# Attention prologue of a two-layer-type kernel: loads of x first on one queue, LayerNorm ahead of the head moves, mask rows filled by token halves, four PSUM banks in one ring

## The chip, the cores and the metric

The kernel runs on one NeuronCore of a Trainium2 chip. A core has engines that run their own instruction streams: TensorE (PE, matmuls and transposes), VectorE (DVE), ScalarE (ACT), GpSimd (POOL) and SyncE (SP, which here only issues DMAs). They meet through semaphores. PE reads SBUF and writes PSUM, which has eight banks of 2 KB per partition. DMAs are issued from the queues of SP, ACT and POOL and share 16 DMA engines. The metric is device time in microseconds (us), median of several runs.

## The reference, cut to what matters

x has 2048 tokens of 576 features. Four layers, A, B, A, B, each added to x. A is attention over a sliding dilated window: 32 heads of 18 features, each token sees the tokens 0, 2, 4, ... 14 behind it. B is a gated MLP that mixes tokens with a 2048 x 2048 matrix; the change does not touch it.

```python
def _A_ref(x, wqkv, wo):
    ...
    W, dil = (8, 2)
    qkv = (lambda x, *d: x.transpose(*d))((x @ wqkv).reshape(B, S, 3, H, Dh), 2, 0, 3, 1, 4)
    q, k, v = (qkv[0], qkv[1], qkv[2])
    ...
    idx = pos[:, None] - off[None, :]
    mask = idx >= 0
    ...
    logits = jnp.einsum('bhsd,bhswd->bhsw', q, kg) * scale
    logits = jnp.where(mask[None, None, :, :], logits, -1000000000.0)
    attn = _softmax(logits, axis=-1)
    o = jnp.einsum('bhsw,bhswd->bhsd', attn, vg)
    return (lambda x, *d: x.transpose(*d))(o, 0, 2, 1, 3).reshape(B, S, D) @ wo
...
x = x + _A_ref(_layernorm(x, axis=-1), A_wqkv, A_wo)
x = x + _B_ref(_layernorm(x, axis=-1), B_w_in, B_w_sp, B_b_sp, B_w_out)
```

(and the last two lines a second time). Inputs and output are bf16.

## The kernel before

Layers are numbered 0 to 3; 0 and 2 are A, 1 and 3 are B. An A layer is written out by hand: inside `manual_schedule` (L336) each engine runs its instructions in the order in which the program makes them. Tokens come in 16 tiles of 128. The normalised x is kept transposed in `xnT` (features on partitions, 16 padding columns in front).

**Stages of an A layer.**
- LayerNorm. In layer 0, `x_load` brings x in as bf16, four tiles at most in a load (tiles 8 to 11 into memory of `oT`, under the name `spare`, the last four into the buffer of the first four). `LNX_stats` takes two bn_stats and one aggregate per tile on VectorE, adds eps, and lets GpSimd raise it to the power -0.5 (L505). `LNX_apply` writes (x - mean) * rstd on VectorE into one of four buffers `ln_xn` (L513). Tiles 0 to 3 are transposed on PE (L518) and copied by ScalarE, the rest by DMA transposes on SP (`ln_T`, L245). Before them, 40 matmuls of an identity by itself (`warm`, L493) run on PE. In layer 2, x was normalised at the end of layer 1.
- `VW(t, hh)` makes half of the values of one of 19 query tiles of 112 tokens: five matmuls of 288 columns, evacuated into `v_ext` (L361).
- `PG(d, qk, cc)`, a projection group, makes q (qk 0) or k (qk 1) of seven heads (four for d = 4) for 512 tokens `cc`: five matmuls of 512 columns into a PSUM bank `pp` (L383), evacuated by ScalarE or VectorE into a staging buffer `stg` (L353, L355). When the four parts of a `stg` (q and k, two cc) are there, one DMA per head moves its 18 rows to that head's place in `QK`: these are the head moves (L392, shown as L77). There are three staging buffers in layer 0, four in layer 2, used in turn; a group can be evacuated only when the moves out of its buffer have landed. The queues of the moves are taken in turn from `q2`, two thirds GpSimd and one third SP.
- The window is imposed by adding rows to q and k: each head has 32 partitions in `QK`, 18 of features and 14 of a pattern with a period of 256 tokens. `build_window_rows` makes a period, sends it through DRAM (`win_period`) into `win_pat`, and `fill_window_rows` copies it over all of `QK` on VectorE, two of eight head groups at a time; the head moves then write over 18 of each 32 rows, so they come after the fill.
- Attention runs in 38 steps `s`, two per query tile (half of the heads each): `L_mm(s)`, 16 logits matmuls into two double banks (`L_ps`, L407), `EXP(s)` on ScalarE (L416), `PV(s)`, 16 matmuls into a bank `O_ps` (L427), a reciprocal and a product on VectorE into `o_t`, and every second step a DMA transpose on SP into `oT` (L438). A table says what else is issued at which step: the remaining groups and values, `WO(i, hh)` (the output projection, bank `pw`, L453), the store of x, LayerNorm for layer B, and loads of B's weights. L_mm(s + 1) and EXP(s + 1) are issued before PV(s).

**PSUM.** Four banks are two double banks `H` (logits). Of the other four, two carry the tag `O` (O_ps) and two the tag `PT` (pp, pv, pw); users that don't mind take the two tags in turn (`PT_tile`, L194). A tile waits for whoever had its bank last.

**Order in layer 0's prologue.** x of tiles 0 to 7 on SP; the weights of v, then of q and k (`wqk`) on ACT's queue; window rows; identity; warm matmuls; LayerNorm of tiles 0 to 3, VW of three tiles, LayerNorm of 4 to 7, loads of x for 8 to 15, the whole fill, then ten pairs of groups (the first 1024 tokens), with LayerNorm of tiles 8 to 11 after the fourth pair and of 12 to 15 after the fifth. Then four more groups (tokens 1024 to 1535 of d = 0, 1, L588) and L_mm(0).

**Order in layer 2.** The ten pairs of groups, with the fill and `setup_bufs` (zeroing padding of `P_sb` and `o_t` on GpSimd, ones into `v_ext` on ScalarE) after the first; VW(0); four groups; L_mm(0).

Memory comes from stacks of pools: `main` first, then `sb`. The staging buffers are in `sb`. A tile that takes memory of an earlier one waits until that one has been read for the last time.

Of the kernel before, what the change touches and what calls it, by code (L numbers as in the profile page):

```python
# [18 lines left out]
P = 128  # L19
D = 576  # L20
H = 32
# [41 lines left out]
class K:  # L63
# [24 lines left out]
    def setup(self):  # L88
# [18 lines left out]
        self.pt_rr = 0  # L107
# [8 lines left out]
    def build_window_rows(self, c):  # L116
# [8 lines left out]
        self.pat = self.consts.tile([P, 2, 256], bf16, name="win_pat")  # L125
# [41 lines left out]
        self.dma(one[:].rearrange("a r (p f) -> p (a r) f", f=16), R[0:16].rearrange("p a r f -> p (a r) f"))  # L167

        def load(eng):
            for j in range(4):  # L170
                self.dma(self.pat[32 * j + DH:32 * j + 32, :, :], one[:].rearrange("a r x -> r a x"), eng=eng)
# [10 lines left out]
    def fill_window_rows(self, QK, g0, g1):  # L182
        nc, S, n = self.nc, self.cfg.S, g1 - g0
        for a in range(2):
            nc.vector.tensor_copy(out=QK[:, a, g0:g1, 0:S].rearrange("p g (k x) -> p g k x", x=256),
                                  in_=self.pat[:, a, None, None, :].to_broadcast([P, n, S // 256, 256]))
            nc.vector.tensor_copy(out=QK[:, a, g0:g1, S:S + PADL],
                                  in_=self.pat[:, a, None, 0:PADL].to_broadcast([P, n, PADL]))
        nc.vector.tensor_copy(out=QK[:, 1, g0:g1, 0:PADL], in_=self.patpad[:, None, :].to_broadcast([P, n, PADL]))
# [4 lines left out]
    def PT_tile(self, shape, dt, name, any_bank=True):  # L194
        self.pt_rr += 1
        tag = "O" if any_bank and self.pt_rr % 2 else "PT"
        return self.ps.tile(shape, dt, name=name, tag=tag, bufs=2)

    def O_tile(self, shape, dt, name):
        return self.ps.tile(shape, dt, name=name, tag="O", bufs=2)  # L200
# [113 lines left out]
    def layer_A(self, li):  # L314
# [9 lines left out]
        qT, kT = QK[:, 0], QK[:, 1]  # L324
        v_ext = main.tile([P, NT, H, DH + 1], bf16, name="v_ext")
# [18 lines left out]
        def setup_bufs():  # L344
            for pb in P_bufs:
                nc.gpsimd.memset(pb[:, :, :, QT:P], 0.0)
            for ob_ in o_bufs:
                nc.gpsimd.memset(ob_[:, D:640], 0.0)
            nc.scalar.copy(out=v_ext[:, :, :, DH:DH + 1], in_=self.ones[:, None, None, :].to_broadcast([P, NT, H, 1]))
# [7 lines left out]
        def VW(t, hh, dve):  # L357
            nk = tdim(t)[0]
            pv = self.PT_tile([P, 512], f32, "pv", any_bank=False)
# [6 lines left out]
        NSTG = 3 if li == 0 else 4  # L366
        CBW = 1024
        dma_rr = [0]

        def PG(d, qk, cc, dve, queues=(nc.sync, nc.gpsimd)):  # L370
# [4 lines left out]
            if key not in stg_tiles:  # L375
                stg_tiles[key] = sb.tile([P, 2, CBW], bf16, name="stg", tag="stg", bufs=NSTG)
                stg_left[key] = 2 * (CBW // 512)
            stg = stg_tiles[key]
            pp = self.PT_tile([P, 512], f32, "pp", any_bank=False)
# [39 lines left out]
        def PV(s):  # L419
            t, hf = divmod(s, 2)  # L420
            nk, nq = tdim(t)
            O_ps = self.O_tile([P, 512], f32, "O_ps")
# [23 lines left out]
        def WO(i, hh):  # L446
# [4 lines left out]
            pw = self.PT_tile([P, 512], f32, "pw", any_bank=False)  # L451
# [20 lines left out]
        if li == 0:  # L472
# [12 lines left out]
            self.load_wqk(nc.scalar)  # L485
            x_load(x1[:, 0:4, :], 4, 4, nc.sync)
            self.zero_right()
            self.build_window_rows(sb)
            self.load_pat(nc.sync)
            self.make_ident()  # L490
            warm = self.PT_tile([P, 512], f32, "warm", any_bank=False)
            for _ in range(40):
                nc.tensor.matmul(warm[:, 0:P], lhsT=self.ident[:], rhs=self.ident[:], start=True, stop=True)  # L493
            setup_bufs()

            def LNX_stats(i0, n):
                mv = sb.tile([P, 4, 2], f32, name="lnx_mv", tag="lnx_mv", bufs=2)
                for k_ in range(n):
# [34 lines left out]
            for t in range(3):  # L533
                for hh in range(2):
                    VW(t, hh, False)
# [426 lines left out]
```

The softmax here doesn't subtract the row's maximum and nothing guards it: scores larger than these inputs give would overflow.

## Time and profile before

| | us |
|---|---|
| median of 7 runs | 1234.35 |
| lowest, highest | 1233.11, 1239.22 |
| profiled execution, its own time | 1234.35 |
| its span, first to last instruction | 1232.5 |
| PE busy in it | 1195.5 |
| mean granted PE clock | 0.993 |

Busy time by stretch of the span, from a view that cuts it into windows (0 to 160 is layer 0, 160 to 625 layer 1, 625 to 762 layer 2, the rest layer 3):

| stretch, us | length | PE busy | PE clock | DMA share |
|---|---|---|---|---|
| 0 to 47 | 47 | 36.00 | 0.96 | 0.66 |
| 47 to 60 | 13 | 8.77 | 0.87 | 0.50 |
| 60 to 125 | 65 | 57.49 | 0.97 | 0.88 |
| 125 to 165 | 40 | 39.53 | 1.00 | 0.80 |
| 165 to 640 | 475 | 472.81 | 1.00 | 0.25 |
| 640 to 665 | 25 | 21.93 | 0.87 | 0.29 |
| 665 to 705 | 40 | 37.14 | 1.00 | 0.90 |
| 705 to 762 | 57 | 54.70 | 1.00 | 1.02 |
| 762 to 805 | 43 | 43.00 | 1.00 | 1.06 |
| 805 to 1140 | 335 | 335.00 | 1.00 | 0.04 |
| 1140 to 1232.5 | 92.5 | 89.12 | 1.00 | 0.36 |

Times are us, and ns where a line says mean. PE stands for matmuls, PEld for the loading of weights, SPq for SP's queue. "L383" is the line of the kernel. "pp<-xnT,wqk_sb" reads: written tile, then what was read. A time in brackets with an arrow is the idle time of that engine before the instruction and what ended it; "issue" means that nothing in the profile shows what it waited for. The DMA share is the mean busy share of the 16 DMA engines.

### The profile page before, as it was taken

How to read it: one execution, taken by the hardware profiler on the slowest of the kernel's cores; microseconds unless marked ns; L12 is line 12 of the kernel's file. 1: busy time of each engine (PE TensorE's matmuls, PEld its weight loads, DVE VectorE, ACT ScalarE, POOL GpSimd, SP SyncE). 2: the span in 40 equal slices, each digit the busy share in tenths (PEclk: the TensorE clock that was granted, in tenths of full speed). 3: DMA queues.
4: the chain of work that ended last, by engine and by line, in shares of the span. 5: the costliest groups of instructions: out<-in, count | busy, mean ns of one | idle time of the engine just before them, and what ended most of it. 6: DMA issues, size and time to landing. Idle time of an engine off the chain costs nothing. (4 is left out here: it accounts for less than half of the span.)

```text
span 1232.5 us, 20796 instructions
## 1 busy us (share of the span) xinstructions
PE 1195.5 (97%) x8568; PEld 623.8 (51%) x8568; DVE 545.4 (44%) x1206; ACT 385.4 (31%) x605; POOL 275.8 (22%) x380
## 2 busy tenths in 40 slices
PE   7789999999999999999999999999999999999998
PEld 4346744444444444447754576444444444444577
DVE  8347867533332322334453577674332232332321
ACT  5457867501011011101146586772001101111000
POOL 3447676300000000001152577751000000000000
PEclk9899999999999999999998999999999999999999
DMA  6688987000000000046644898920000000000432
GB/s 181 110 158 189 198 188 166 22 1 11 11 11 12 1 11 11 1 154 191 173 102 96 179 229 178 243 60 22 1 11 11 11 11 11 12 1 2 135 109 73
DMA packets 176149, 101.58 MB, mean 82 GB/s; under 512 B 134954, under 2 KB 156506, under 8 KB 176054
## 3 DMA queue, kind: packets, MB, share of 16 engines
q1 hardware_dynamic: 163814, 76.04, 28.0%
q0 software_dynamic: 6896, 18.39, 5.9%
q10 hardware_dynamic: 5344, 5.83, 1.5%
q8 instruction: 67, 1.10, 0.4%
q14 instruction: 28, 0.23, 0.1%
HBM read 42.39 MB, written 16.53 MB: 48 GB/s over the span
## 5 line engine op out<-in xcount | busy, mean ns | idle before, releaser
L795 PE MATMUL pg<-Wq,Z 128*128 128x512 bf16 x2304 | 502.8, 379 | 0.0
L795 PEld LDWEIGHTS <-Z 128*128 128x128 bf16 x2304 | 225.7, 98 | 271.6
L799 DVE TENSOR_TENSOR g_tmp<-pg,ln_xn 128x512 f32<-128x512 f32 x144 | 99.6, 692 | 429.1 <-PE pg L795 429.1
L789 ACT ACTIVATE z1T<-pz 128x1024 bf16<-128x1024 f32 x72 | 73.7, 1024 | 513.8 <-PE pz L777 513.6
L849 PE MATMUL po<-wout,Z 128*128 128x288 bf16 x1152 | 141.4, 286 | 0.0
L77 POOL DMA_DIRECT2D wout<-in_B_w_out_dram x4 | 4.3, 1064 | 604.6 <-PE pg L795 604.6
L416 ACT ACTIVATE P_sb<-L_ps 128x896 bf16<-128x896 f32 (+1 forms) x152 | 126.4, 887 | 41.3 <-PE L_ps L407 40.7
L777 PE MATMUL pz<-xnT,w 128*128 128x512 bf16 (+1 forms) x640 | 136.0, 380 | 0.0
L849 PEld LDWEIGHTS <-Z 128*128 128x128 bf16 x1152 | 112.7, 98 | 28.8
L700 PEld LDWEIGHTS <-xnT 128*128 128x128 bf16 (+1 forms) x800 | 66.3, 97 | 81.9 <-issue 24.5
L383 PE MATMUL pp<-xnT,wqk_sb 128*128 128x512 bf16 x400 | 98.5, 397 | 6.7 <-ACT stg L355 4.0
L700 PE MATMUL pz<-win2a,xnT 128*128 128x512 bf16 x384 | 104.4, 380 | 0.0
L800 DVE TENSOR_TENSOR Z<-g_tmp,z1T 128x512 bf16<-128x512 f32 x144 | 99.7, 692 | 9.7
L777 PEld LDWEIGHTS <-w 128*128 128x128 bf16 (+1 forms) x640 | 51.1, 97 | 80.0 <-issue 27.1
L714 ACT ACTIVATE zp<-pz 128x1024 bf16<-128x1024 f32 x64 | 65.5, 1024 | 44.9 <-PE pz L700 32.4
L238 POOL TENSOR_SCALAR ln_xn<-x_new,ln_mv,ln_rstd 128x576 bf16<-128x576 f32 x32 | 73.3, 2290 | 3.4
L859 DVE TENSOR_TENSOR x_new<-po,xo 128x288 f32<-128x288 f32 (+1 forms) x64 | 28.8, 456 | 87.8 <-PE po L849 87.8
L700 PE MATMUL pz<-win2b,xnT 128*128 128x512 bf16 (+1 forms) x256 | 65.7, 380 | 0.0
L383 PEld LDWEIGHTS <-wqk_sb 128*128 128x128 bf16 x400 | 38.3, 101 | 52.3 <-issue 16.4
L77 POOL DMA_DIRECT2D QK<-stg x74 | 48.4, 657 | 64.3 <-issue 26.1
L716 DVE CUSTOM_DVE_ANT_0 Z<-zp 128x1536 bf16<-128x1536 bf16 x32 | 56.9, 1779 | 11.2 <-ACT zp L714 11.2
L453 PE MATMUL pw<-wo_sb,oT 128*128 128x288 bf16 x320 | 49.1, 286 | 11.7 <-issue 4.8
(103 smaller groups left out, 903.2 us busy)
## 6 DMA issues: line engine op xcount, KB each, us to landing
xres<-x_new SPq DMA_DIRECT2D x48, 288.0 KB
xo<-xres SPq DMA_DIRECT2D x48, 288.0 KB
QK<-stg POOLq DMA_DIRECT2D x74, 72.0 KB, 3.9
wout<-in_B_w_out_dram POOLq DMA_DIRECT2D x4, 1296.0 KB, 9.4
w<-in_B_w_in_dram SPq DMA_DIRECT2D x16, 256.0 KB
QK<-stg SPq DMA_DIRECT2D x54, 72.0 KB
win2a<-in_B_w_in_dram POOLq DMA_DIRECT2D x12, 288.0 KB, 5.4
wqk_sb<-in_A_wqkv_dram ACTq DMA_DIRECT2D x2, 1152.0 KB
```

The lines of the kernel that those rows point to most:

```text
L238: e.tensor_scalar(out=xn[:nrows, 0:D], in0=x_t[:nrows, :], scalar1=mv[:nrows, 0:1], scalar2=rstd[:nrows, 0:1], op0=ALU.subtract, op1=ALU.mult)
L383: nc.tensor.matmul(pp[:, :], lhsT=w, rhs=self.xnT[:, c, PADL + cc * 512:PADL + (cc + 1) * 512], start=(c == 0), stop=(c == 4))
L416: nc.scalar.activation(out=P_bufs[(2 * s + jp) % 4][:nk, :, :, 0:nq], in_=Lv[:nk, :, :, 0:nq], func=ACT.Exp, scale=scale)
L700: nc.tensor.matmul(pzvs[ci][:, sub * 512:sub * 512 + w], lhsT=self.xnT[r0:r1, c, PADL + i * P:PADL + (i + 1) * P], rhs=win2(c)[r0:r1, c0 + ...
L714: nc.scalar.activation(out=zp[:, c0:c0 + cn], in_=pzvs[ci][:, 0:cn], func=ACT.Gelu_apprx_tanh, accum_out=sums[:, ci:ci + 1])
L716: nc.vector.tensor_tensor_reduce(out=spare[:, 0:SQ_D], in0=zp[:, 0:SQ_D], in1=zp[:, 0:SQ_D], scale=1.0, scalar=0.0, op0=ALU.mult, op1=ALU. ...
L777: nc.tensor.matmul(pz1s[q // 2][:, q % 2, :], lhsT=w1[r0:r1, c, sub * P:(sub + 1) * P], rhs=self.xnT[r0:r1, c, PADL + q * 512:PADL + (q + ...
L789: nc.scalar.activation(out=z1T[:, q2 * 512:(q2 + 2) * 512], in_=pz1s[q2 // 2][:, :, :].rearrange("p a b -> p (a b)"), func=ACT.Gelu_apprx_ ...
L795: nc.tensor.matmul(pg[:, :], lhsT=Z[:, jj, i, sub * P:(sub + 1) * P], rhs=Wq[q][:, i, :], start=(i == 0), stop=(i == NS - 1))
L799: nc.vector.tensor_tensor(out=tmp[:], in0=pg[:, :], in1=bsp[:, qs], op=ALU.add)
L800: nc.vector.tensor_tensor(out=uT(jj)[:, sub, qs], in0=tmp[:], in1=z1Ts[jj, sub][:, qs], op=ALU.mult)
L849: nc.tensor.matmul(acc[hh], lhsT=uT(j // 2)[:, j % 2, i * P:(i + 1) * P], rhs=wouts[j // NJH][:, j % NJH, hh * 288:(hh + 1) * 288], start= ...
```

## The change

- Loads: `wqk` moves from ACT's queue to SP, behind the x of tiles 0 to 7; x of tiles 8 to 11 comes next, ahead of the window pattern; x of 12 to 15 after the apply of tiles 4, 5. `win_period` is sent from ACT's queue. `load_wo` moves from step 1 to the prologue.
- LayerNorm of layer 0 is cut into statistics (S_), eps (E_), power on GpSimd (R_), apply (A_), transpose (T_pe, T_) and issued by hand, tile by tile. Statistics of all 16 tiles, and all but the power, apply and transpose of the last four, stand ahead of the groups; the power of tiles 12 to 15 comes after d = 1's head moves. `warm` has 26 matmuls.
- The fill is cut into two halves of 1024 tokens: the second is issued after the fifth pair of groups (layer 0) or the seventh (layer 2). A copy covers four head groups; the pattern gets a tail of 16 columns.
- Head moves of the first half in layer 0: d = 0, 1, 4 on GpSimd alone; d = 2, 3 on GpSimd and SP in turn.
- pp, pv, pw, O_ps and all other single-bank users share one ring of four banks.
- Staging buffers lie in `main`, behind `QK`.
- Groups of the second half: two, not four, come early, after EXP(0) and evacuated by VectorE; the other 18 are spread over 14 steps. VW of tiles up to 6 (layer 0) or 3 (layer 2) stand ahead of L_mm(0). WO of tiles 0 to 2 in layer 0 comes two steps later. B's first weights are loaded from step 4, not 2.
- An Exp of one column (`exp_table`) early in each A layer loads ScalarE's table; layer 2's `setup_bufs` and the ones of `v_ext` run on VectorE.

```diff
-        self.dma(one[:].rearrange("a r (p f) -> p (a r) f", f=16), R[0:16].rearrange("p a r f -> p (a r) f"))
+        self.dma(one[:].rearrange("a r (p f) -> p (a r) f", f=16), R[0:16].rearrange("p a r f -> p (a r) f"), eng=eng)
...
-    def fill_window_rows(self, QK, g0, g1):
...
+    def fill_window_rows(self, QK, half):
+        nc, n = self.nc, self.cfg.S // 2
+        if half == 0:
+            nc.vector.tensor_copy(out=self.pat[:, :, 256:272], in_=self.pat[:, :, 0:16])
+            nc.vector.tensor_copy(out=QK[:, 0, :, 0:PADL], in_=self.pat[:, 0, None, 0:PADL].to_broadcast([P, 8, PADL]))
+            nc.vector.tensor_copy(out=QK[:, 1, :, 0:PADL], in_=self.patpad[:, None, :].to_broadcast([P, 8, PADL]))
+        c0 = PADL + half * n
+        for g0 in (0, 4):
+            for a in range(2):
+                nc.vector.tensor_copy(out=QK[:, a, g0:g0 + 4, c0:c0 + n].rearrange("p g (k x) -> p g k x", x=256),
+                                      in_=self.pat[:, a, None, None, PADL:PADL + 256].to_broadcast([P, 4, n // 256, 256]))
...
+    def PT_tile(self, shape, dt, name):
+        return self.ps.tile(shape, dt, name=name, tag="PT", bufs=4)
...
+        stgs = [main.tile([P, 2, CBW], bf16, name=f"stg{k_}") for k_ in range(NSTG)]
...
+        def exp_table():
+            nc.scalar.activation(out=P_bufs[0][:, 0, 0, 0:1], in_=self.ones[:, 0:1], func=ACT.Exp)
...
             self.load_wv(nc.scalar)
-            self.load_wqk(nc.scalar)
             x_load(x1[:, 0:4, :], 4, 4, nc.sync)
+            self.load_wqk(nc.sync)
             self.zero_right()
+            exp_table()
...
+            x_load(spare, 8, 4, nc.sync)
             self.load_pat(nc.sync)
...
+            S_(0, 1)
+            E_(0, 2)
+            R_(0, 2)
+            S_(2)
+            A_(0, 1)
+            T_pe(0)
+            T_pe(1)
+            VW(0, 0, False)
+            VW(0, 1, False)
+            S_(3)
+            E_(2, 2)
+            R_(2, 2)
+            VW(1, 0, False)
+            VW(1, 1, False)
+            S_(4)
+            A_(2, 3)
+            T_pe(2)
+            T_pe(3)
+            S_(5)
+            E_(4, 2)
+            R_(4, 2)
+            VW(2, 0, False)
+            VW(2, 1, False)
+            S_(6)
+            A_(4, 5)
+            x_load(sb.tile([P, 4, D], bf16, name="x_in3", tag="x_in", bufs=2)[:], 12, 4, nc.sync)
+            T_(4, 5)
+            S_(7)
+            E_(6, 2)
+            R_(6, 2)
+            A_(6, 7)
+            T_(6, 7)
+            self.load_wo(nc.gpsimd)
+            self.fill_window_rows(QK, 0)
+            S_(8, 9, 10, 11)
+            E_(8, 4)
+            R_(8, 4)
+            A_(8, 9, 10, 11)
+            T_(8, 9, 10, 11)
+            S_(12, 13, 14, 15)
+            E_(12, 4)
             order = [(d, cc) for cc in (0, 1) for d in (0, 1, 2)] + [(d, cc) for d in (3, 4) for cc in (0, 1)]
             for k_, (d, cc) in enumerate(order):
                 for qk in (1, 0):
-                    PG(d, qk, cc, False, q2)
+                    PG(d, qk, cc, False, (nc.gpsimd, nc.sync) if 2 <= d <= 3 else (nc.gpsimd,))
                 if k_ == 4:
+                    R_(12, 4)
+                    A_(12, 13, 14, 15)
+                    self.fill_window_rows(QK, 1)
                 if k_ == 7:
+                    T_(12, 13, 14, 15)
+            nvw0, nvw = 3, 7
         else:
...
                 if k_ == 0:
+                    setup_bufs(nc.vector)
+                    nc.vector.memset(v_ext[:, :, :, DH:DH + 1], 1.0)
+                    self.fill_window_rows(QK, 0)
+                    exp_table()
                 if k_ == 1:
                     self.run_deferred()
+                if k_ == 6:
+                    self.fill_window_rows(QK, 1)
+            nvw0, nvw = 0, 4
...
+        for t in range(nvw0, nvw):
             for hh in range(2):
+                VW(t, hh, False)
...
-        for d, qk, cc in pgs[:4]:
-            PG(d, qk, cc, False, q2)
-        pgs = pgs[4:]
+        pre, pgs = pgs[:2], pgs[2:]
...
-            s = 2 * t + (4 if t < NT - 3 else 3)
+            s = 2 * t + (6 if li == 0 and i < 3 else 4 if t < NT - 3 else 3)
...
-            at(2 + 2 * k_, f)
+            at(4 + 2 * k_, f)
...
         L_mm(0)
         EXP(0)
+        for d, qk, cc in pre:
+            PG(d, qk, cc, True, q2)
```

## The prediction, made before the changed kernel had run

> **What bounds the kernel now.** I read the busy shares first, then the chain of waits, then what TensorE waits for, then TensorE, ScalarE and GpSimd in order of time around the two attention layers.
>
> ```profile
> PE 1195.5 (97%) x8568; PEld 623.8 (51%) x8568; DVE 545.4 (44%) x1206; ACT 385.4 (31%) x605; POOL 275.8 (22%) x380
> PE 42%; DMA 1%; DVE 0%; issue 0%; ACT 0%
> ```
>
> TensorE (PE) is the bound: 37 us idle in 1232.5. The change leaves the matmuls of the answer as they are, so it can only win idle time, or time in which a matmul ran at half pace. Both lie almost wholly in the two A layers (0 to 160 us, 625 to 762 us). PE's waits from 0 to 125 us (total, times, longest), and below them ScalarE's from 0 to 60 us:
>
> ```profile
> PE pw L453 <- issue: 4.8, 1, 4.8
> PE pp L383 <- ACT stg L355: 4.0, 2, 2.1
> PE L_ps L407 <- ACT P_sb L416: 3.4, 4, 2.3
> PE pw L453 <- DVE stg L353: 2.0, 7, 0.5
> PE L_ps L407 <- DMA QK<-stg: 1.5, 1, 1.5
> ACT stg L355 <- DMA QK<-stg: 8.8, 4, 3.0
> ```
>
> The last line explains the second and third: ScalarE can't empty a PSUM bank into a staging buffer whose head moves have not landed; behind that evacuation PE runs out of banks, and EXP(0) queues. The moves are late because GpSimd, which issues two thirds of them, sits in front of a LayerNorm power op:
>
> ```profile
> 26.55 3.15 POOL L77 DMA_DIRECT2D QK<-stg  x4 [9.55 <-ACT stg L355]
> 32.12 1.03 POOL L505 TENSOR_TENSOR lnx_rstd<-lnx_rstd,neg_half 128x4 f32<-128x4 f32 x1 [2.42 <-DVE lnx_rstd L504]
> 33.12 3.03 POOL L77 DMA_DIRECT2D QK<-stg  x5
> 38.74 1.04 POOL L505 TENSOR_TENSOR lnx_rstd<-lnx_rstd,neg_half 128x4 f32<-128x4 f32 x1 [2.59 <-DVE lnx_rstd L504]
> ```
>
> Idle time is paid twice, since the granted clock falls after it. Two projection groups (PG, five 512-column matmuls each, 1.08 us at full clock) should take 2.16 us. PE in order of time (start, length, what, idle before it) behind the first logits of each A layer, and before layer 2's:
>
> ```profile
> 54.75 3.75 PE L383 MATMUL pp<-xnT,wqk_sb 128*128 128x512 bf16 x10
> ...
> 629.41 19.87 PE L383 MATMUL pp<-xnT,wqk_sb 128*128 128x512 bf16 x90 [2.07 <-DVE stg L353]
> ...
> 657.95 0.37 PE L407 MATMUL L_ps<-QK 32*128 32x112 bf16 x8 [2.58 <-ACT P_sb L416]
> ...
> 659.69 4.43 PE L383 MATMUL pp<-xnT,wqk_sb 128*128 128x512 bf16 x10
> ```
>
> One microsecond of the first (length, PE busy, clock, DMA), then what ScalarE did in the 2.58:
>
> ```profile
> 55.00:56.00 1.00, 1.00 (x4) 0.50 0.00 0
> ```
>
> ```profile
> 655.68 1.28 ACT L416 ACT_TABLE_LOAD   x1
> ```
>
> **Layer 0, up to the first logits L(0).** Before, L(0) starts at 48.82 with 24 PG and 6 VW behind it. After, 20 PG and 14 VW precede it (8 x 0.61 = 4.88 us in place of 4 x 1.08 = 4.32: 0.56 more work).
>
> Start: x goes ahead of wqk. Before, tile 4 reached VectorE at 11.81, and the first apply began at 9.05 because both statistics pairs came first. After: statistics of tiles 0, 1 end at 6.44, the power at 7.45, tile 2's at 7.6, then the two applies: 1.45 us sooner. So PG starts at about 14.65, not 16.15. wqk now stands behind 1.18 MB of x; at the 370 to 380 GB/s of 6.6 to 9.6 us it lands near 11, in time.
>
> VectorE: nothing idle, tiles 4 to 7 are applied by 16.9; the first fill half (4 copies x 1.22 + 3 small x 0.17 = 5.4) ends at 22.4; four statistics (0.97 each) at 26.3; GpSimd's power of tiles 8 to 11 (1.03) ends at **27.5**. That power stands ahead of every head move on GpSimd. Before, the first move went at 26.55. Then 7 moves of d=0 and 7 of d=1, all on GpSimd at 0.61: issued by 31.8 and 36.0, landed (median 3.9, here 3.4 as with d=0 before) at 35.2 and 39.5. The power of tiles 12 to 15 now comes behind d=1's moves and blocks none of these. SP takes four transposes of tiles 8 to 11 (1.33 each, to 33.3) before its half of d=2 and d=3.
>
> PE: 12 PG end at 27.6; d=3's evacuation waits for d=0's landing at 35.2. The ring of four banks lets four more PG run, to 31.9; the 17th waits for the first freed bank, 35.85: **3.95 us idle**, as much as the 1.87 + 2.10 of before, in another place. I add 1.95 for the halved clock after it (before: 30 matmuls from 40.53 in 8.36, not 6.5). PG 17 to 20 end at 42.2, eight VW at 47.1. So L(0) comes at 47.1: 1.7 earlier with 0.56 more done, **2.3 won**. Ends: no stall at all, L(0) at 41.1 (8 won); all GpSimd moves at 0.82 and landing in 5.5 (its longest), 5 to 8 lost against the 2.3.
>
> **L(0) to PV(0).** Before: 48.82 to 54.75, of which 1.3 is work; 4.6 idle. After, two PG of the second token half stand between L(0) and L(1), and d=4's four moves (evacuated 42.8, issued to 45.2 or 46.4, landed 49 to 51) are needed at 49.6. I keep 0.5: **4.1 won**. The two PG behind it run at full clock: 3.75 - 2.16 = **1.6**.
>
> **WO(0).** Its 4.80 ("issue") ends at 77.58. wo had landed by 72.1 (issued 62.2 to 63.0, landing 8.6 to 9.1), so it was the transpose of o_t issued at 68.12, amid DMA shares of 1.0 to 1.3. After, WO of tiles 0 to 2 comes two steps later, wo is loaded in the prologue, and the weights for B start two steps later: PV(3) near 58, its transpose issued near 61, needed near 71.7. I cost the wait at nothing: 4.80, and 1.26 of slow clock (3.42 for ten at 79.31): **6.1**.
>
> **Four banks for all.** pw waited 0.17 and 0.43 alternately for pp's evacuation, because pp, pv and pw turned on two banks. With four, pw takes the bank of four allocations ago, a step old: **2.0 in each A layer**. O_ps loses its own pair, but its bank too is a step old.
>
> **Layer 2.** The 2.07 at 629.41: the staging buffers lay where layer B's last tiles live; now they are allocated beside QK, under Z, which PE has finished with: **2.07**. The buffers' memsets go from GpSimd to VectorE and now lie over those tiles, so they wait for ln_xn to 628.64; with memsets 0.8, v_ext ones (128x608; between 0.3, by L280, and the 2.83 of ScalarE's copy; I take 0.6, a memset being nearer to a memset) and 5.4 of fill, d=0's moves start at 635.5, not 632.4. d=4 needs their buffer at 643.6; they land at 643. Covered, barely. The Exp table load goes from the path at 655.68 to 628, beside PE. L(1) falls near 654, d=4's moves land by 654: of 2.58 + 0.44 I keep 0.5: **2.5**. Clock: 4.43 - 2.16 + 1.41 - 0.61 = **3.07**. The 1.06 at 681.56 for oT I leave in: without VW in steps 0 to 5 it has less cover, and may grow by 1.
>
> Two rules of the Trainium skill speak against this change.
>
> "TensorE: Matmul & The Clock Gate" (What you observe) has the array at half rate until some 4 us of sustained matmuls. Row: the 40 warm matmuls took 267 to 314 ns each, the transposes directly behind them 216 to 220. 26 at 0.11 end at 8.5. By the rule the transposes and first VW run slow, up to 1.7 us later; by my sum it costs nothing, as PE then waits 3.95 for moves that don't depend on it. Clock records say 1.0 here, so durations decide.
>
> "SBUF — State Buffer" (Who interferes with whom) lets a two-port VectorE copy lock GpSimd out for its whole length. Rows: 4 moves in 3.15 (0.79) beside fill copies, 5 in 3.03 (0.61) without. Full locking would give each move up to 1.22. The second fill (38.5 to 43.4) runs beside some eight moves: 8 x 0.18 = 1.4 by the rows, up to 5 by the rule. I take the rows; the 0.5 at L(1) stands for it.
>
> **Sum.** Layer 0: 2.3 + 4.1 + 1.6 + 6.1 + 2.0 = 16.1. Layer 2: 2.07 + 2.5 + 3.07 + 2.0 = 9.6. 1232.5 - 25.7 = 1206.8; the profiled execution lasted 1234.35, 1.85 beyond its span, and is itself the median. Forecast **1208.6**.
>
> **Rivals.**
> - *GpSimd's queue becomes the wait* (0.22): moves at 0.8 and landing at 5.5, so d=3, d=4 and L(1) are late. For: all of d=0, 1 and 4 on one queue behind the 27.5; the locking rows. Against: the queue is free of powers from 27.5 to 36. 8 us back: 1216.6.
> - *The stall at 31.9 does not come* (0.14): the first moves start at about 24, right after d=0's evacuation. For: x8 to x11 come early, and bn_stats is the only thing in front. Against: the power's place in the queue. 3.95 + 1.95 + 0.5 more: 1202.2.
> - *The change misses WO(0)* (0.10): the DMA engines are already over 1.0 from 64 to 80, so the transpose is just as late two steps on. 6 back: 1214.7.
> - *Slower* (0.03): one ring ties O_ps to VectorE. Where two PG fall in a step, VectorE empties two pp (0.69 each), O_ps (0.72) and pw in order; if PE then waits on a bank in each of 76 steps, 0.34 us a step eats the 25.7. At 0.45 us a step: 1208.6 + 34.2 = 1242.8. Against: VectorE needs some 2.6 in a 3.2 us step.
>
> The likeliest case has 0.51; its own range is 1203 to 1214. The range for 8 in 10 is 1198 to 1222. A measurement of this kernel tells about 0.3% (3.7 us) from no change: faster 0.95, same 0.02, slower 0.03.
>
> **What would show it.** Right: PG from about 14.7; first head move at 27.5; one PE idle of about 4 us near 32 with half clock behind it; no wait of pw on stg; no table load between L(0) and EXP(0) in layer 2; PE unbroken from 625 on. Wrong: L(1) waiting over 2 us on moves, WO(0) still waiting, or O_ps waiting for banks.

## The result, and the profile after

| | before | after |
|---|---|---|
| median, runs | 1236.74, 36 | 1229.58, 15 |
| lowest, highest | 1231.81, 1240.24 | 1225.13, 1238.47 |
| profiled execution, its own time | 1234.35 | 1225.29 |
| its span | 1232.5 | 1223.5 |
| layer 0 ends (first 256-column matmul `pzs` of layer 1) | 159.89 | 161.63 |
| layer 2, first projection group to the same matmul | 138.81 | 127.82 |

After over before is 0.9951, 95% interval 0.9935 to 0.9968: faster, by a quarter of what was forecast (1208.6, range 1198 to 1222). The profiled execution is among the shortest of the 15 runs after, so the two profiles differ by 9.0 us where the medians differ by 7.2. Of the 9.0, layer 2 brings 11.0 (9.6 forecast), and layer 0 **loses 1.7** (a gain of 16.1 forecast). So the miss lies in layer 0.

The busy times after. TensorE still is the bound, with 31.7 us idle, not 37.

```profile
PE 1191.8 (97%) x8554; PEld 623.1 (51%) x8554; DVE 549.7 (45%) x1203; ACT 378.9 (31%) x599; POOL 277.2 (23%) x377
```

TensorE's waits after, from 0 to 125 us (total, times, longest):

```profile
PE pp L383 <- DMA xnT<-ln_xn: 4.4, 1, 4.4
PE pv L362 <- ACT stg L356: 2.6, 1, 2.6
PE pw L453 <- DVE x_new L456: 2.1, 1, 2.1
PE pv L362 <- DVE o_t L434: 1.4, 2, 1.1
PE pv L362 <- DVE x_new L456: 1.3, 1, 1.3
PE pp L383 <- ACT stg L356: 1.1, 1, 1.1
```

The old names are gone (pw by "issue", pw by stg, L_ps by moves), and two new ones have come: xnT from a DMA transpose in the prologue, and x_new, the output of the attention layer, behind it. Where the new waits sit, TensorE in order of time after, up to the groups behind PV(0):

```profile
14.83 6.64 PE L383 MATMUL pp<-xnT,wqk_sb 128*128 128x512 bf16 x30
25.84 12.64 PE L383 MATMUL pp<-xnT,wqk_sb 128*128 128x512 bf16 x50 [4.37 <-DMA xnT<-ln_xn]
39.56 4.48 PE L383 MATMUL pp<-xnT,wqk_sb 128*128 128x512 bf16 x20 [1.08 <-ACT stg L356]
46.61 6.73 PE L362 MATMUL pv<-wv_sb,xnT 128*128 128x288 bf16 x40 [2.57 <-ACT stg L356]
53.27 0.40 PE L407 MATMUL L_ps<-QK 32*128 32x112 bf16 x16
...
56.61 2.32 PE L383 MATMUL pp<-xnT,wqk_sb 128*128 128x512 bf16 x10
```

After six groups TensorE stands 4.37 us for the transposes of tiles 4 to 7. Its 50 matmuls behind that take 12.64 where full pace is 10.8, and the 40 of VW 6.73 where they take 5.06 in layer 2. The granted clock in the profile is 0.50 from 26.6 to 29.9 us and from 47.1 to 50.4, that is, behind the stops of 4.37 and 2.57; behind the one of 1.08 it is 1.00. L(0) comes at 53.27, not 47.1. The two groups behind PV(0), 3.75 before, now run at full clock. GpSimd after, which issues the moves:

```profile
26.07 1.04 POOL L512 TENSOR_TENSOR lnx_rstd<-lnx_rstd,neg_half 128x4 f32<-128x4 f32 x1 [8.48 <-DVE lnx_rstd L509]
30.53 6.01 POOL L77 DMA_DIRECT2D QK<-stg  x10 [3.42 <-ACT stg L356]
...
40.58 10.89 POOL L77 DMA_DIRECT2D QK<-stg  x11
```

The power was done at 27.11, as forecast; the first move did not go then but waited 3.42 us more for the evacuation of d = 0, which TensorE's stop had made late. The last line has 11 moves in 10.89 us, though a move takes 0.6: one of them took 4.89. The stops of 1.08 and 2.57 come from the landing of the moves: ScalarE stood before the evacuations of d = 3 and of d = 4 until the moves out of their buffers, those of d = 0 and d = 1, had landed:

```profile
38.92 2.05 ACT L356 CAST stg<-pp 128x512 bf16<-128x512 f32 x4 [4.14 <-DMA QK<-stg]
45.97 2.06 ACT L356 CAST stg<-pp 128x512 bf16<-128x512 f32 x4 [4.99 <-DMA QK<-stg]
```

The gap behind layer 0's early part is shown best by SP's queue after:

```profile
77.93 3.42 SPq L77 DMA_DIRECT2D xo<-in_A_x_dram  x2
81.39 1.23 SPq L438 DMA_TRANSPOSE oT<-o_t  x1
87.15 0.33 SPq L77 DMA_DIRECT2D xo<-in_A_x_dram  x1
87.53 3.74 SPq L77 DMA_DIRECT2D QK<-stg  x4
91.32 0.46 SPq L77 DMA_DIRECT2D xres<-x_new  x1
```

From 82.62 to 87.15 SP does nothing: the load of xo for tile 4 stands first in its queue and waits for its buffer, which tile 1's second add (VectorE, 86.67 to 87.13) sets free. Behind it stand four head moves and, at 91.32, the first store of x_new. VectorE in turn waits for such stores, since there are three x_new buffers, and TensorE for VectorE:

```profile
96.32 0.77 PE L453 MATMUL pw<-wo_sb,oT 128*128 128x288 bf16 x5 [2.14 <-DVE x_new L456]
```

The waits of VectorE and of SP, 75 to 135 us, the leading line of each:

```profile
DVE x_new L456 <- DMA xres<-x_new: 8.3, 2, 5.5
```

```profile
SPq L77 <- DVE ln_st L211: 14.0, 4, 5.1
```

Before the change SP lost 3.9 us in that way. A third wait has grown: from 60 us to the end of layer 0, pw stands 3.8 us in all for transposes of o_t into oT (0.5 before, the 4.80 of WO(0) not counted). And layer 2 after, TensorE from its first group on, and the table load of ScalarE:

```profile
626.77 21.75 PE L383 MATMUL pp<-xnT,wqk_sb 128*128 128x512 bf16 x100
...
657.09 0.59 PE L407 MATMUL L_ps<-QK 32*128 32x112 bf16 x10 [0.40 <-DMA QK<-stg]
...
658.03 2.32 PE L383 MATMUL pp<-xnT,wqk_sb 128*128 128x512 bf16 x10
```

```profile
630.41 1.28 ACT L350 ACT_TABLE_LOAD   x1
```

A hundred matmuls without a break, the table loaded beside them, 0.6 us of waiting for moves at L(1), and full clock behind PV(0).

### The profile page after: what moved, and what is told of

Read it like the earlier page. It is cut to its first block, busy times and chain, and to the rows that moved or that the text cites. A ratio compares the mean times of both kernels' runs of the same rounds, so it can differ in the third digit from the quotient of the medians.

```text
span 1223.5 us, 20740 instructions
## 1 busy us (share of the span) xinstructions
PE 1191.8 (97%) x8554; PEld 623.1 (51%) x8554; DVE 549.7 (45%) x1203; ACT 378.9 (31%) x599; POOL 277.2 (23%) x377
## 4 chain that ended last, share of the span: by engine, by line
PE 88%; DMA 4%; POOL 4%; issue 2%; DVE 1%; SPq 1%; ACT 0%; POOLq 0%; DVEq 0%
PE pg L825 41%; PE pz L807 12%; PE po L879 12%; PE pz L730 10%; PE pp L383 5%; POOL ln_xn L235 2%; PE pv L362 2%; PE pw L453 2%; PE O_ps L427 2%; PE pzs L730 1%; DMA oT<-o_t 1%; PE L_ps L407 1%; DMA QK<-stg 1%; POOL ln_rstd L216 1%; DMA xnT<-ln_xn 0%
## 5 line engine op out<-in xcount | busy, mean ns | idle before, releaser
L819 ACT ACTIVATE z1T<-pz 128x1024 bf16<-128x1024 f32 x72 | 73.7, 1024 | 513.8 <-PE pz L807 513.6
L383 PE MATMUL pp<-xnT,wqk_sb 128*128 128x512 bf16 x400 | 93.5, 384 | 5.5 <-DMA xnT<-ln_xn 4.4
L744 ACT ACTIVATE zp<-pz 128x1024 bf16<-128x1024 f32 x64 | 65.5, 1024 | 45.7 <-PE pz L730 32.3
L77 POOL DMA_DIRECT2D QK<-stg x78 | 53.5, 688 | 57.9 <-DVE stg L354 43.6
L362 PE MATMUL pv<-wv_sb,xnT 128*128 128x288 bf16 (+1 forms) x380 | 58.9, 296 | 6.0 <-ACT stg L356 2.6
L383 PEld LDWEIGHTS <-wqk_sb 128*128 128x128 bf16 x400 | 37.1, 98 | 47.1 <-DMA xnT<-ln_xn 4.8
```

The source lines that it names most:

```text
L362: nc.tensor.matmul(pv[:nk, 0:288], lhsT=self.xnT[:, c, QT * t:QT * t + nk], rhs=wv_sb[:, c, hh * 288:(hh + 1) * 288], start=(c == 0), stop ...
L383: nc.tensor.matmul(pp[:, :], lhsT=w, rhs=self.xnT[:, c, PADL + cc * 512:PADL + (cc + 1) * 512], start=(c == 0), stop=(c == 4))
L744: nc.scalar.activation(out=zp[:, c0:c0 + cn], in_=pzvs[ci][:, 0:cn], func=ACT.Gelu_apprx_tanh, accum_out=sums[:, ci:ci + 1])
L819: nc.scalar.activation(out=z1T[:, q2 * 512:(q2 + 2) * 512], in_=pz1s[q2 // 2][:, :, :].rearrange("p a b -> p (a b)"), func=ACT.Gelu_apprx_ ...
```

## The experiments

In the table "ratio" compares all runs of a kernel with all runs of the kernel before on the same chip, with its 95% interval; it lies near the ratio of the means, so it can differ a little from that of the medians. The other columns are from one profiled execution each (us): first head move on GpSimd, first logits L(0), first PV(0), end of layer 0, length of layer 2. "WO early" and so on are the names used below.

| kernel | median | ratio | first move | L(0) | PV(0) | layer 0 ends | layer 2 |
|---|---|---|---|---|---|---|---|
| before | 1236.74 | 1 | 26.55 | 48.82 | 54.30 | 159.89 | 138.81 |
| after | 1229.58 | 0.9951 (0.9935 to 0.9968) | 30.53 | 53.27 | 56.19 | 161.63 | 127.82 |
| 1 WO early | 1218.85 | 0.9881 (0.9827 to 0.9936) | 28.37 | 50.84 | 57.51 | 152.64 | 128.08 |
| 2 loads late | 1230.07 | 0.9951 (0.9930 to 0.9972) | 26.99 | 48.72 | 56.95 | 164.71 | 129.33 |
| 3 both | 1219.53 | 0.9877 (0.9838 to 0.9915) | 26.93 | 50.36 | 55.25 | 153.67 | 131.25 |
| 4 old layer 0 | 1223.66 | 0.9905 (0.9874 to 0.9937) | 26.70 | 49.56 | 54.99 | 159.18 | 126.80 |
| 5 XO late | 1219.93 | 0.9859 (0.9818 to 0.9900) | 32.45 | 51.14 | 56.34 | 150.62 | 131.74 |
| 6 fill first | 1222.23 | 0.9883 (0.9861 to 0.9904) | 30.69 | 53.35 | 57.66 | 154.64 | 132.09 |
| 7 fill, loads | 1213.73 | 0.9820 (0.9794 to 0.9847) | 25.29 | 49.03 | 53.37 | 150.62 | 128.98 |
| 8 fill, queues | 1226.56 | 0.9922 (0.9896 to 0.9947) | 30.88 | 47.75 | 59.43 | 159.82 | 132.37 |
| 9 all | 1214.92 | 0.9854 (0.9828 to 0.9879) | 25.37 | 49.33 | 52.25 | 147.98 | 131.47 |
| 10 d1 split | 1214.13 | 0.9850 (0.9798 to 0.9901) | 25.86 | 43.40 | 49.80 | 149.02 | 127.00 |
| 11 two tags | 1225.15 | 0.9929 (0.9904 to 0.9955) | 29.51 | 56.03 | 59.52 | 159.07 | 135.95 |
| 12 W early | 1219.45 | 0.9839 (0.9796 to 0.9882) | 31.12 | 49.39 | 56.18 | 155.54 | 128.90 |

The changed kernel and kernels 1 to 10 and 12 run the same code in layer 2 and differ there by up to 5.6 us (126.8 to 132.4). So the experiments are compared by layer 0's columns; these too come from single executions, and a difference under some 5 us in the end of layer 0, or of two or three in a median, is not proof of anything by itself.

**1, WO early.** The two-step shift of WO in layer 0 undone.

```diff
-            s = 2 * t + (6 if li == 0 and i < 3 else 4 if t < NT - 3 else 3)
+            s = 2 * t + (4 if t < NT - 3 else 3)
```

> Edit: output projection of tiles 0 to 2 in layer 0 back at the step of before (no shift by two). Theory S (the shift holds SP's queue: the load of xo for tile 3 stands in it waiting for tile 0's buffer, and the store of x, the moves and the transposes wait behind it): the waits of PE between 88 and 112 us of the changed kernel on x_new and o_t (2.1, 1.1, 0.6, 1.3) go; layer 0 ends 6 to 10 us sooner, less a wait of 0 to 4 us at the first output projection. Rival B (the shared ring of four banks couples O_ps, pv and pw to VectorE): these waits stay at 4 us or more, the end of layer 0 moves by less than 2 us.

The waits on x_new go, and layer 0 ends 9.0 us sooner although PV(0) comes 1.3 later. Ratio 0.9881 against 0.9951; the intervals just touch. WO(0) comes at 74.77 and does not wait: the shift was not needed for it.

**2, loads late.** x of tiles 12 to 15 is loaded behind the transposes of tiles 4 to 7, and wo at step 1.

```diff
-            x_load(sb.tile([P, 4, D], bf16, name="x_in3", tag="x_in", bufs=2)[:], 12, 4, nc.sync)
...
             T_(6, 7)
-            self.load_wo(nc.gpsimd)
+            x_load(sb.tile([P, 4, D], bf16, name="x_in3", tag="x_in", bufs=2)[:], 12, 4, nc.sync)
...
+            at(1, self.load_wo, nc.gpsimd)
```

> Edit: x of tiles 12 to 15 is loaded behind the transposes of tiles 4 to 7 on SP, wo at step 1 as before. Theory L (the two loads, 1.2 MB, take the DMA engines from the transposes of tiles 4 to 7): the transposes land by 22.5 to 23.5, PE's wait before the seventh group falls from 4.4 to under 2 us, the halved clock behind it goes (2 us), the first logits come 3 to 6 us earlier than at 53.3. Rival Q (the transposes are late by their own number and issue time): the wait stays at 3.5 us or more and the first logits at 52 or later.

The wait for xnT falls from 4.4 to 1.0 and L(0) comes 4.5 sooner: the loads were what the transposes waited for. But PV(0) comes at 56.95, the end of layer 0 no sooner and the median is unchanged; the head moves, waited for at L(1) four times and 4.4 us in all, took it back, and the blocked queue of SP is still there.

**3, both** edits together.

> Both edits of the two kernels above. Theories S and L together: layer 0 ends 9 to 16 us sooner than in the changed kernel, the time is 0.7 to 1.3% below it (near 1215 to 1221 where the changed kernel has 1230). If only one holds, it equals the better of the two within 2 us.

PV(0) 55.25, layer 0 at 153.67: no better than the first alone. What is won at the first wait comes back as a stop of 4.96 us for staging buffers, whose moves have not landed.

**4, old layer 0.** Layer 0's prologue (but for the fill's larger copies), early groups, WO and weight loads as before the change; the ring of four banks, the staging buffers and layer 2 as after. Of the edit, the end:

```diff
+        if li == 0:
+            for d, qk, cc in pgs[:4]:
+                PG(d, qk, cc, False, q2)
+            pre, pgs = [], pgs[4:]
+        else:
+            pre, pgs = pgs[:2], pgs[2:]
...
+            at((2 if li == 0 else 4) + 2 * k_, f)
```

> Edit: layer 0's prologue, its early groups, its output projection and its weight loads as before; ring of four banks, staging buffers beside QK, and all of layer 2 as in the changed kernel. Theory (layer 2 brings all of the gain, layer 0 loses what it wins): layer 2 takes 127 to 129 us from its first group to the first 256-column matmul of layer 3 as in the changed kernel (before: 138.8), layer 0 ends 1 to 3 us sooner than before by the ring alone, so the time is 12 to 14 us below before, and better than the changed kernel by 3 to 7. Rival (the gain of layer 2 leans on the new layer 0, for example through the weights' loads or the memory of the pools): layer 2 takes 132 or more.

Layer 0 ends 0.7 us before the old one, layer 2 takes 126.8, and the ratio, 0.9905, is under that of the whole change. Layer 2 and the ring bring all that the change brings; what is new in layer 0 takes some of it away. Kernel 1 says which part: it has all of the new prologue, only not the shift of WO, and its layer 0 ends 6.5 us sooner than here. This kernel also has WO(0)'s old wait:

```profile
77.77 1.36 PE L453 MATMUL pw<-wo_sb,oT 128*128 128x288 bf16 x5 [4.72 <-issue]
```

**5, XO late.** The shift of WO stays, and the loads of xo for tiles 3 to 5 are shifted with it.

```diff
-            at(s - 5, XO, i)
+            at(s - 5 + (2 if li == 0 and 3 <= i < 6 else 0), XO, i)
```

> The changed kernel with the two-step shift of WO(0..2) kept, and the loads XO(3..5) of layer 0 put two steps later as well, so that SP meets them when their buffers are already free. Theory S (SP's queue stood at xo loads whose buffers WO(0..2) still held, and with it the stores that free x_new): the waits of pw, pv and O_ps on x_new between 85 and 165 (5.3 us in the changed kernel) fall under 1.5, TensorE waits under 4 in all there, layer 0 ends at 153 to 156, time 1220 to 1224. Rival (what costs is that WO(2) and WO(3) now fall into one step, three x_new buffers for four open tiles): the waits on x_new stay over 3 us, layer 0 ends at 159 to 162, time 1227 to 1231.

SP's queue in this kernel, from the xo load for tile 3 to the first store:

```profile
81.20 0.51 SPq L77 DMA_DIRECT2D xo<-in_A_x_dram  x1
83.56 3.75 SPq L77 DMA_DIRECT2D QK<-stg  x4
87.36 0.45 SPq L77 DMA_DIRECT2D xres<-x_new  x1
```

The moves go 4 us sooner, and so does the store; VectorE's wait for stores falls from 8.3 to 0.3. The stretch 85 to 112 us (length, busy time of PE, PEld, DVE, ACT and POOL with counts, clock, DMA share, GB/s), first after, then here:

```profile
85.00:112.00 27.00, 20.41 (x324) 13.82 (x322) 16.03 (x48) 14.81 (x20) 19.23 (x21) 1.00 0.69 161
```

```profile
85.00:112.00 27.00, 26.26 (x464) 18.29 (x461) 21.65 (x64) 20.68 (x29) 23.62 (x27) 1.00 1.01 218
```

TensorE works 5.85 us more of the 27, and the DMA engines are busier, not freer: it was order, not load. Layer 0 ends at 150.62, 11.0 sooner than after, below the 153 expected. That tiles 2 and 3 meet in one step, the rival, is the same as after and leaves no wait of TensorE on x_new.

**6, fill first.** On the first kernel (WO early): both halves of the mask fill ahead of the statistics of tiles 8 to 11, the powers behind the moves of d = 0 and of d = 2.

```diff
             self.fill_window_rows(QK, 0)
+            self.fill_window_rows(QK, 1)
             S_(8, 9, 10, 11)
             E_(8, 4)
-            R_(8, 4)
...
-                if k_ == 4:
+                if k_ == 3:
+                    R_(8, 4)
+                    A_(8, 9, 10, 11)
+                    S_(12, 13, 14, 15)
+                    E_(12, 4)
+                if k_ == 5:
+                    T_(8, 9, 10, 11)
                     R_(12, 4)
                     A_(12, 13, 14, 15)
-                    self.fill_window_rows(QK, 1)
```

> Base: the changed kernel without the shift of WO (1218.85). Both halves of the mask fill are done before the statistics of tiles 8 to 11, and the two powers on GpSimd stand behind the moves of d = 0 and of d = 2, so that no large copy lies beside head moves. Theory K (a fill copy locks GpSimd out: one move took 5.3 us, and it delayed d = 4): no move takes over 1.4 us, the last of d = 4 is issued 4 to 5 us sooner, the wait of L_ps on moves (2.6) goes, PV(0) at 52 to 54 instead of 57.5, layer 0 ends near 149, time 1214 to 1216. Rival M (the moves are bound by their landing on the DMA engines, median 6.1, not by GpSimd): the lock goes, but landing stays over 6 and PV(0) comes at 56 to 58; 1217 to 1220.

GpSimd's head moves, first after (38 to 48 us), then here (durations in ns: shortest, median, longest):

```profile
L77 POOL DMA_DIRECT2D QK<-stg x9: 593/593/4886, 37.7 to 47.9; - x9
```

```profile
L77 POOL DMA_DIRECT2D QK<-stg x25: 593/596/677, 30.7 to 50.5; - x25
```

The long move is gone with the copies. In after it began at 41.86 and lasted until the four copies (4.63 us, 42.02 to 46.65) were over; the same is seen in kernels 1, 5, 11 and 12 (4.88 to 5.30). But it does not follow from the copies alone: in kernels 2 and 3 moves run beside the same four copies back to back and wait for about one copy each. Kernel 3, 20 to 60 us:

```profile
L77 POOL DMA_DIRECT2D QK<-stg x25: 587/590/1390, 26.9 to 48.8; - x25
```

What decides is open; kernels 2 and 3 differ from the five in that their loads come late. PV(0) stays at 57.66, so neither theory holds as put: the moves of layer 0's prologue land sooner (median 4.9, against 7.0 in the first kernel), yet they start 2.3 us later than there, and TensorE waits 4.3 at VW for staging buffers instead.

**7, fill and loads.** The last with the loads late.

> As the last, and with the load of x12 to x15 behind the transposes of tiles 4 to 7 and wo loaded at step 1. Theory K: with no lock behind it, the 3.4 us that TensorE wins at the first wait (groups resume at 22.5, not 25.4) reach PV(0), at 50 to 52; time 1212 to 1214. Rival M: the moves start sooner and land later, PV(0) within 1 us of the last kernel's; time the same as its within 2 us.

Layer 0's hundred prologue matmuls run in one piece:

```profile
15.56 21.77 PE L383 MATMUL pp<-xnT,wqk_sb 128*128 128x512 bf16 x100
42.70 6.39 PE L362 MATMUL pv<-wv_sb,xnT 128*128 128x288 bf16 x40 [5.37 <-ACT stg L356]
```

The first move goes at 25.29, PV(0) is 4.3 sooner than in the sixth, and the median of 1213.73 is the lowest of all here (ratio 0.9820, interval clear of the sixth's). Late loads gained nothing in the median in kernel 3 against the first, and 8.5 us here against the sixth. That suggests that the early moves and the early fill need each other, but it is not shown: by PV(0) late loads gain 2.3 without the early fill and 4.3 with it; layer 2, the same code in both, is itself 3.1 shorter in this profile; and the interval overlaps those of kernels 1 and 3. The stop of 5.37 that is left is again the landing of d = 1's moves.

**8, fill and queues.** The sixth with the moves of every d on GpSimd and SP in turn.

```diff
-                    PG(d, qk, cc, False, (nc.gpsimd, nc.sync) if 2 <= d <= 3 else (nc.gpsimd,))
+                    PG(d, qk, cc, False, (nc.gpsimd, nc.sync))
```

> As the fill-first kernel, with the head moves of all d in layer 0's prologue split between GpSimd and SP instead of d = 0, 1 and 4 on GpSimd alone. Theory Q (one queue issues too slowly, 7 x 0.6 = 4.2 us for a d): d = 0's moves are all landed 1 to 2 us sooner, the first evacuation of d = 3 at 37 to 38, time 1 to 3 us under the fill-first kernel's. Rival: an issue on SP takes 1.2 to 1.4 us here against GpSimd's 0.6, so half of seven on SP takes as long as all seven on GpSimd: the same within 1.5 us.

Slower by 4.3 us in the median, though the intervals overlap; layer 0 ends 5.2 later. L(0) is early (47.75), as fewer moves stand on GpSimd, but PV(0) is the latest but one of all. SP's queue:

```profile
47.46 3.02 SPq L77 DMA_DIRECT2D QK<-stg  x3
50.59 5.18 SPq L242 DMA_TRANSPOSE xnT<-ln_xn  x4
55.86 1.65 SPq L77 DMA_DIRECT2D QK<-stg  x2
```

Two of d = 4's moves stand behind four transposes of tiles 12 to 15 that nobody needs yet. L(1) waits 5.0 us for them. Both theories looked at the rate of issue; what the trace shows is again who stands in front on SP.

**9, all.** Fill, late loads, shift of WO with its late xo.

> The changed kernel with the shift of WO kept, XO(3..5) two steps later, the whole mask fill ahead of the head moves, and the load of x12 to x15 and of wo behind the transposes of tiles 4 to 7. Theory S and K together: the parts lie in different stretches (up to PV(0): 53.4 in the kernel with fill and loads; behind it: waits of 2.4 in the kernel with the late XO), so they add: the waits of pw on oT fall from 4.4 to about 1.5, layer 0 ends near 148, time 1210 to 1212. Rival: with PV(0) at 53 SP's queue meets the xo loads earlier than their buffers are free again, or oT is late however late WO comes; layer 0 at 150 to 152, time 1213 to 1216.

Missed. The wait of pw on oT falls to 2.4 in layer 0, which ends at 147.98, as expected, but the median is not below the seventh's, and the two intervals overlap. Its layer 2, the same code, took 131.47 in the profile. Whether the shift adds anything to the seventh isn't settled.

**10, d1 split.** The last with d = 1's moves on both queues.

```diff
-                    PG(d, qk, cc, False, (nc.gpsimd, nc.sync) if 2 <= d <= 3 else (nc.gpsimd,))
+                    PG(d, qk, cc, False, (nc.gpsimd, nc.sync) if 1 <= d <= 3 else (nc.gpsimd,))
```

> As the last, with the seven moves of d = 1 split between GpSimd and SP, whose queue is idle then. Theory Q (d = 4's evacuation, which TensorE waits 5.4 us for, stands behind the landing of d = 1's moves, and these behind d = 0's seven and a power on one queue): d = 1 is issued 1.5 to 2 us sooner, the 5.4 falls to 3 to 4, L(0) 1.5 to 2 us sooner, time 1 to 2 us under the last kernel's. Rival (the landing on the DMA engines decides, or SP's later transposes now hold up d = 2's half): the wait stays at 5 or comes back at L(1); within 1 us of the last kernel, or slower.

TensorE's waits from 0 to 60 us:

```profile
PE pp L383 <- DMA xnT<-ln_xn: 2.3, 2, 1.3
PE L_ps L407 <- DMA QK<-stg: 1.7, 1, 1.7
...
PE pp L383 <- ACT stg L356: 0.5, 1, 0.5
```

The 5.2 of the ninth at VW is gone, 0.5 for a staging buffer is left before a group, and L(0) comes at 43.40, 5.9 sooner, three times what was expected; PV(0) 2.4 sooner. At layer 0's end nothing is left of it: two stops near 100 us (1.07 by x_new, 0.72 by oT) are followed by half clock (0.50 from 101.5 to 108.2). Its four runs spread from 1209.2 to 1226.51: the wait is explained, the gain is unclear.

**11, two tags.** The fifth (XO late) with the ring taken apart: O_ps on two banks, pt, pp, pv and pw of the A layers on the other two.

```diff
-        return self.ps.tile(shape, dt, name=name, tag="PT", bufs=4)
+        self.pt_rr = getattr(self, "pt_rr", 0) + 1
+        o = name == "O_ps" or name in ("pzs", "pg", "po") and self.pt_rr % 2
+        return self.ps.tile(shape, dt, name=name, tag="O" if o else "PT", bufs=2)
```

> The changed kernel with XO(3..5) two steps later (1219.93), and the four banks taken apart again: O_ps on two of its own, pt, pp, pv and pw of layer A on the other two. Theory R (the ring of four banks removes the waits of pw for the evacuation in front, 7 times 0.17 to 0.47 in each A layer, and lets TensorE run on in the prologue): these waits come back, 2 us in each A layer, and 1 to 2 us more in the prologue; time 1224 to 1227. Rival (without the stall that led to them the waits don't come back, or they only move slack about): 1219 to 1222.

TensorE's waits from 0 to 60 us, then from 600 to 765:

```profile
PE pp L385 <- ACT stg L358: 5.4, 1, 5.4
```

```profile
PE pw L455 <- DVE stg L356: 1.9, 7, 0.4
```

The ring is worth 5.2 us in the median (1225.15 against 1219.93; the intervals, from 0.9904 and to 0.9900, just part). In layer 2 the seven waits of pw are back with 1.9 us, the 2.0 of the sum; in layer 0 only 0.6 is. The largest new stop is the one of 5.4 in the prologue. The profile of this kernel is the slowest of its runs (1230.39), so its columns make the loss look larger than the median does.

**12, W early.** The first with B's weights from step 2 again.

```diff
-            at(4 + 2 * k_, f)
+            at(2 + 2 * k_, f)
```

> The changed kernel without the shift of WO (1218.85), with B's first weights loaded from step 2 again, as before the change, not from step 4. Theory W (the transpose that WO(0) needs was late because two weight loads were issued just ahead of it, at 66.2 against 68.1, so moving the loads and not the shift of WO cured the 4.80): with the loads issued ahead of the transpose again, WO(0) waits 3 to 5 us, layer 0 ends at 155 to 158, time 1222 to 1225. Rival (the wait came of the moves and groups in front: twice the groups ahead of it, wo's own load at 62, and these are gone): WO(0) waits under 1 us, layer 0 ends at 152 to 154, time 1217 to 1220.

WO(0) waits 0.22:

```profile
74.69 0.77 PE L453 MATMUL pw<-wo_sb,oT 128*128 128x288 bf16 x5 [0.22 <-PE pp L383]
```

So neither the shift (1), nor wo's own load (3, at step 1 again), nor this one is by itself what removed the 4.80. The fourth kernel brings it back with all of layer 0's old order; which part of that holds it stays open.

## Why the prediction was wrong

**The step that failed: "WO of tiles 0 to 2 comes two steps later ... I cost the wait at nothing".** The sum booked the 6.1 us that go and nothing for the move itself. The wait at WO(0) did go (WO(0) at 77.19 has none), but not by the shift: kernels 1, 3 and 12 have no shift and wait there 0.22 at most. And the shift also moves the adds that free the xo buffers by two steps, while the loads of xo for tiles 3 to 5 stay where they were on SP's in-order queue. They stood there for 14.0 us, the stores of x_new stood behind them, VectorE behind the stores (8.3), and TensorE behind VectorE. Taking either side away, the shift (kernel 1) or the lag of the loads (kernel 5), brings layer 0's end 9.0 and 11.0 us forward and the ratio from 0.9951 to 0.9881 and 0.9859 (some 9 and 11 us; the interval of kernel 5 is clear of the changed kernel's, that of kernel 1 touches it).

From PV(0) to the end of layer 0 the kernel before took 105.6 us. By the sum it should have been about 93: less 9.7 (1.6 + 6.1 + 2.0), and less 2.7 for work now done ahead of PV(0) (eight VW more, two groups fewer). The changed kernel took 105.4, kernel 5 94.3. So once the loads move with the shift, this part of the sum comes out; the step accounts for some 11 of the 17.8 us that layer 0 lacks, and the delay at PV(0), below, for most of the rest. The trace of before had the wait in sight: SP stood from 81.60 to 84.81 in front of an xo load, and the code has three buffers.

```profile
80.28 1.32 SPq L438 DMA_TRANSPOSE oT<-o_t  x1
84.81 0.35 SPq L77 DMA_DIRECT2D xo<-in_A_x_dram  x1
```

The prediction looked at GpSimd's queue for the moved power and at SP's for four transposes, and asked of WO only what it waits for, not who waits for it.

**"PE: 12 PG end at 27.6".** The twelfth is evacuated from 34.20 on, 6.6 us late. The sum had tiles 4 to 7 applied by 16.9 (17.1 came) and let the groups run through without a wait for their transposes. It left out that the moved loads of x12 to x15 and of wo share the DMA engines with them. From 18 to 22 us (the same columns as in kernel 5; the last but one is the DMA share), after and then kernel 2:

```profile
18.00:22.00 4.00, 3.47 (x17) 1.37 (x14) 4.00 (x5) 2.25 (x4) 0.00 (x0) 1.00 1.20 207
```

```profile
18.00:22.00 4.00, 3.49 (x17) 1.37 (x14) 4.00 (x5) 2.23 (x4) 0.00 (x0) 1.00 0.84 132
```

The wait was 4.4 us, plus about 1.8 of half clock on the 50 matmuls behind. Kernel 2 takes the loads away, and 1.0 is left.

**"landed ... at 35.2 and 39.5".** The forecast stall, "3.95 us idle" near 32, came as two, 1.08 at 39.56 and 2.57 at 46.61: nearly right in sum, but partly by luck. d = 0's moves had landed by 38.9 and d = 1's by 46.0. They started 3.0 us late (30.53, not 27.5), which is most of the first delay of 3.7; the second, 6.5, has as much again from landing: the last of d = 1, issued at 39.0, took about 7 us, where the sum took 3.4. Half clock behind it cost 1.67, as the sum had it (its 1.95 should be 1.86 by its own line, 8.36 less 6.5).

**"8 x 0.18 = 1.4 by the rows, up to 5 by the rule. I take the rows".** Eleven moves took 10.89 us, 4.3 more than at 0.6 each, so the term was mis-sized by 2.9; the size was nearer to that of the rule of the Trainium skill ("SBUF — State Buffer", Who interferes with whom). The rows of before misled: their copies were single, of 1.22 us with small ones in between; the four of the new second half stand back to back. But neither gives the cost: in kernel 3 it was 1.6, beside the same copies. And it is not what the change lost: L(1) did not wait for a move after.

**The clock rule** ("TensorE: Matmul & The Clock Gate", What you observe) was set at nothing and is nearly that: behind 26 warm matmuls the first ten transposes took 1.26 us, the next ten 0.72, and the first 20 of VW 2.62 where 2.53 is full pace, about 0.6 in all of the 1.7 allowed. (The 1.0 that the prediction read there is no measurement: the clock records of that trace begin at 9.9 us.) Groups began at 14.83 (forecast 14.65); in the kernels with the same start they began between 14.75 and 15.62.

**Layer 0 up to PV(0)**: of the 6.4 us booked, 0.8 came. Between L(0) and PV(0) 4.7 was won where 4.1 was booked, but in place of the 2.3 up to L(0) 3.9 was lost, by the stops above. The 1.6 of clock behind PV(0) came as 1.4.

**Layer 2**: right in the parts that can be read. 2.07 gone (groups unbroken from 626.77), table load beside the groups (630.41), 0.6 left at L(1) where 0.5 was kept, full clock behind, no wait of pw on stg. 11.0 won against 9.6 is on the lucky side: over the twelve kernels with the same layer 2 it is 6.4 to 12.0, 9.2 in the mean. What varies most is the wait of pw on oT, 2.1 after and up to 5.3 in the others.

**Rivals.** "GpSimd's queue becomes the wait" named, with its late landing, the next bound after the two above (kernels 7 and 10 show it), but not the main cause here. "The stall at 31.9 does not come": it came. "One ring ties O_ps to VectorE": its sign was there, O_ps waited 0.6 us once for VectorE's add, but as a net loss it is refuted; kernel 11, without the ring, is slower. "The change misses WO(0)" fell. What happened, a load moved by nobody that blocks a queue, was among none of them, and of the three signs of being wrong two did not show and the third, O_ps waiting, came with 0.6 us alone.

## What to carry to other kernels

When work is moved to a later step, also list what it frees, and for each thing freed, which instruction waits for it on which in-order queue; if that one is not moved too, everything behind it on its queue is. A load brought forward into idle time is paid by the transfers that are already there: look up the DMA share of the slice in which it lands, and which small transfer TensorE waits for next. A cure can take away its own wait and win nothing, since the next one stands right behind it (kernels 2 and 6), so a null result of one edit does not clear its cause.

## What the runs showed that was not expected

A move's issue on GpSimd took 0.59 us alone. Beside four VectorE copies back to back (4.63 us) one issue took 4.88 to 5.30 in five kernels, the whole run of copies, and at most 1.55 and 1.39, about one copy, in kernels 2 and 3; why is open.

Four DMA transposes kept TensorE waiting 3.5 to 4.9 us in the seven kernels where 1.2 MB of loads (x12 to x15 and wo) ran beside them, and 1.0 or less in the five where these loads came behind.

Half clock does not go by the length of a stop. In the clock records of the traces it comes in stretches of 3.4 us, now and then 6.8, each short one worth some 1.7 us of work (half of 3.4): behind the stop of 2.57 us 1.67 was lost, behind the one of 4.37 1.84. Not every stop brings one: behind 3.55 us in kernel 1, 50 matmuls took 10.95, and behind 2.70 in kernel 8 ten took 2.33, both full pace.
